# Moving the last stores of a DMA-bound attention backward pass onto chosen DMA engines

## The chip, the cores and the metric

The kernel runs on one core of a Trainium2 chip. The metric is the device time of one execution in microseconds (us); lower is better. Executions of the kernel before on one chip lie within 0.2%. Times in a trace count from the start of the span; the span is about 1.8 us shorter than the time (400.8 against 402.56 us for the profiled run of the kernel before).

## The reference, cut to what matters

The program is the forward and backward pass of one decode step: 32 heads attend over a cache of 4096 keys and values of width 128, beside a small gated MLP. Its outputs include the gradients of both caches, which are as large as the caches.

```python
def _A_ref(x, k_cache, v_cache, wq, wo):          # B, Sq = 1, 1; D = 640
    q = (x @ wq).reshape(B, Sq, H, Dh).transpose(0, 2, 1, 3)
    scores = jnp.einsum("bhqd,bhkd->bhqk", q, k_cache) * (Dh ** -0.5)
    o = jnp.einsum("bhqk,bhkd->bhqd", softmax(scores), v_cache)
    return o.transpose(0, 2, 1, 3).reshape(B, Sq, H * Dh) @ wo
# ... g * A + (1 - g) * B, with B an MLP
# outputs: the result, and d/d(x, k_cache, v_cache, wq, wo, w1, b1, w2, gate_w)
```

K and V are read (32 MB each), dK and dV are written (32 MB each), and the weights and their gradients make up the rest of 165 MB.

## The kernel before

Per head, K and V (1 MB each) are loaded by SyncE, and dK and dV (1 MB each) are stored by GpSimd; the last stores go through SyncE. A DMA "engine" below is one of the core's 16; the traces don't name them. The parts that the change touches:

```python
def ring(h):
    return nc.sync if h >= H - 2 else nc.gpsimd
...
        def dwo():                                   # one of 8 tiles of d(wo), 128 x 5120 B
            for i in range(G):
                nc.vector.tensor_scalar(wos[g][:, i, :], da_bc[:], fs["o4"][:, i:i + 1], None, ALU.mult)
            (nc.sync if g == NG - 1 else nc.gpsimd).dma_start(dwo_v[g], wos[g][:])
...
        if h == H - 1:                               # dK of the last head, in two halves
            a, b = half * (J // 2), (half + 1) * (J // 2)
            ring(h).dma_start(dKv[h][:, a:b, :], st["dK"][:, a:b, :])
...
        if half == 1:
            if h % 7 == 5 and h < H - 3:             # heads 5, 12, 19, 26
                spread(h // 7, dVv[h], st["dV"])
            else:
                ring(h).dma_start(dVv[h], st["dV"][:])

    def spread(i, dst, t):                           # a dV store meant to nearly skip one engine
        ...
        if i % 3 == 0:
            nc.gpsimd.inc_swdge_sem([], [], mode="reset_dge_cursor")
        for a, b in (((120, 125), (0, 120), (125, 128)), ((0, 14), (14, 119), (119, 128)), ((0, 8), (8, 128)))[i % 3]:
            nc.gpsimd.dma_start(out[a:b, :], src[a:b, :], max_dma_last_dim=J * Dh)
...
    nc.sync.dma_start(dwq_v[:, :, CL:], dwq_l[:])    # the last columns of d(wq)
...
    for i, dst in enumerate((out0_rows, out1_rows, out9_rows)):
        nc.scalar.dma_start(dst, fin_rows[i * RC:(i + 1) * RC, :])    # small results, last of all
```

Of the kernel before, what the change touches and what calls it, by code (L numbers as in the profile page):

```python
# [16 lines left out]
def kernel(  # L17
# [24 lines left out]
    nc = tc.nc  # L42
    P = 128
    _, H, Sk, Dh = A_k_cache.shape
# [6 lines left out]
    NG = H // G  # L51
# [15 lines left out]
    dKv = out_2.rearrange("b h (p j) d -> (b h) p j d", p=P)  # L67
    dVv = out_3.rearrange("b h (p j) d -> (b h) p j d", p=P)
    wq_v = A_wq.rearrange("(rc r) c -> r rc c", r=P)
    dwq_v = out_4.rearrange("(rc r) c -> r rc c", r=P)  # L70
    wo_v = A_wo.rearrange("(g p i) n -> g p i n", p=P, i=G)
    dwo_v = out_5.rearrange("(g p i) n -> g p i n", p=P, i=G)
# [26 lines left out]
    def f32v(ap):  # L99
        return ap.bitcast(F32)  # L100

    def bcast_rows(out, cols, n, parts=P):
        for i in range(n):
            nc.tensor.transpose(out[:, i, :], cols[:, i:i + 1].to_broadcast([parts, P]),
                                ident_bf[0:parts, 0:parts])
# [7 lines left out]
    kts, vts, wqs, wos = {}, {}, {}, {}  # L113

    def ring(h):
        return nc.sync if h >= H - 2 else nc.gpsimd
# [132 lines left out]
    def add(name, kind, fn, deps=(), head=0):  # L249
        steps.append((name, kind, fn, tuple(deps), head))  # L250
# [83 lines left out]
    def finish_steps(g):  # L334
        fs = {}

        def om():
            fs["om"] = small.tile([P, G, G], BF16, name="om", tag="om")
            nc.vector.tensor_tensor(fs["om"][:], o_all[:, g * G:(g + 1) * G].unsqueeze(2).to_broadcast([P, G, G]),
                                    mask4[:].to_broadcast([P, G, G]), ALU.mult)  # L340

        def o4():
            fs["ps"] = gr_ps.tile([P, G], F32, name="o4_ps", tag="gr")
            R = P // G
            for hh in range(G):
                nc.tensor.matmul(fs["ps"][hh * R:(hh + 1) * R, :], lhsT=red4[:], rhs=fs["om"][:, hh, :],
                                 start=True, stop=True)

        def o4c():
            fs["o4"] = small.tile([P, G], F32, name="o4", tag="o4")  # L350
            nc.vector.tensor_copy(fs["o4"][:], fs["ps"][:])
            fs["o4b"] = small.tile([P, G], BF16, name="o4b", tag="o4b")
            nc.vector.tensor_copy(fs["o4b"][:], fs["o4"][:])

        def amm():
            fs["ap"] = gr_ps.tile([P, RC], F32, name="ap_ps", tag="gr")
            for c in range(RC):
                for i in range(G):
                    nc.tensor.matmul(fs["ap"][:, c:c + 1], lhsT=wos[g][:, i, c * P:(c + 1) * P],
                                     rhs=fs["o4b"][:, i:i + 1], start=(i == 0), stop=(i == G - 1))  # L360

        def aadd():
            nc.vector.tensor_tensor(a_acc[:], a_acc[:], fs["ap"][:], ALU.add)

        def dwo():
            for i in range(G):
                nc.vector.tensor_scalar(wos[g][:, i, :], da_bc[:], fs["o4"][:, i:i + 1], None, ALU.mult)  # L367
            (nc.sync if g == NG - 1 else nc.gpsimd).dma_start(dwo_v[g], wos[g][:])

        def dqb():  # L370
            b_ps = gr_ps.tile([P, G, P], BF16, name="b_ps", tag="gr")
            bcast_rows(b_ps, dq_all[:, g * G:(g + 1) * G], G)
            nc.scalar.copy(f32v(dq_bc[:, g * GD:(g + 1) * GD]), f32v(b_ps[:].rearrange("p a b -> p (a b)")))

        def dx(rc, c0, c1, slot_i):
            def f():
                w = g // 2
                nc.vector.scalar_tensor_tensor(junk[:, c0:c1], in0=wqs[w][:, rc, c0:c1], scalar=1.0,  # L378
                                               in1=dq_bc[:, w * WG * Dh + c0:w * WG * Dh + c1],
                                               op0=ALU.mult, op1=ALU.mult, accum_out=dxp[:, rc, slot_i:slot_i + 1])  # L380
            return f

        n = lambda x: f"{x}{g}"
        add(n("om"), "T", om)
        add(n("dqb"), "P", dqb)
        add(n("o4"), "P", o4, (n("om"),))
        add(n("o4c"), "T", o4c, (n("o4"),))
        add(n("amm"), "P", amm, (n("o4c"),))
        add(n("aadd"), "T", aadd, (n("amm"),))
        add(n("dwo"), "D", dwo, (n("aadd"),))  # L390
        for rc in range(RC):
            if g >= NG - 2:
                add(n(f"dx{rc}_"), "D", dx(rc, (g % 2) * GD, (g % 2 + 1) * GD, g - NG + 2 + NW - 1), (n("dqb"),))
            elif g % 2 == 1:
                add(n(f"dx{rc}_"), "D", dx(rc, 0, WG * Dh, g // 2), (n("dqb"),))
# [206 lines left out]
    def outer(dst, col, row, half):  # L602
        n = J // 2
        a, b = half * n, (half + 1) * n
        nc.vector.tensor_tensor(  # L605
            dst[:, a:b, :].rearrange("p j (a b) -> p j a b", b=2),
            col[:, a:b, :].unsqueeze(2).to_broadcast([P, n, Dh // 2, 2]),
            row.rearrange("p (a b) -> p a b", b=2).unsqueeze(1).to_broadcast([P, n, Dh // 2, 2]),
            ALU.mult)

    def dk_half(h, half):
        if h < 0:
            return
        st = sts[h]
        if half == 0:
            st["dK"] = outs.tile([P, J, Dh], BF16, name="dK_sb", tag="dVK")
        outer(st["dK"], st["ds"], gps[h // G]["qd"][:, 0, (h % G) * Dh:(h % G + 1) * Dh], half)
        if h == H - 1:
            a, b = half * (J // 2), (half + 1) * (J // 2)
            ring(h).dma_start(dKv[h][:, a:b, :], st["dK"][:, a:b, :])  # L620
        elif half == 1:
            ring(h).dma_start(dKv[h], st["dK"][:])  # L622
        if half == 1:
            sts.pop(h)

    def dv_half(h, half):
        st = sts[h]
        if half == 0:
            st["dV"] = outs.tile([P, J, Dh], BF16, name="dV_sb", tag="dVK")
        outer(st["dV"], st["p"], gps[h // G]["qd"][:, 1, (h % G) * Dh:(h % G + 1) * Dh], half)  # L630
        if half == 1:
            if h % 7 == 5 and h < H - 3:
                spread(h // 7, dVv[h], st["dV"])
            else:
                ring(h).dma_start(dVv[h], st["dV"][:])  # L635

    def spread(i, dst, t):
        src = t[:].rearrange("p j d -> p (j d)")
        out = dst.rearrange("p j d -> p (j d)")
# [5 lines that stand above are left out]
    def period(h):  # L645
# [12 lines left out]
        def o_part(a, b):  # L658
            for j in range(a, b):
# [4 lines left out]
        nc.vector.reduce_max(m32[:], S, axis=AX.X)  # L664
        V(0)
        dk_half(h - 1, 0)
        V(1)
        nc.tensor.transpose(MM, m32[:].to_broadcast([P, P]), ident_f[:])
        negM = small.tile([P, 1], F32, name="negM", tag="negM")
        nc.vector.tensor_reduce(negM[:], MM, axis=AX.X, op=ALU.max, negate=True)  # L670
        dk_half(h - 1, 1)
        e = st["e"] = small.tile([P, J], BF16, name="e_bf", tag="e_bf")
        V(2)
# [17 lines left out]
        nc.vector.scalar_tensor_tensor(pj[:], in0=DP[:, 0:J], scalar=1.0, in1=e[:], op0=ALU.mult, op1=ALU.mult,  # L691
                                       accum_out=part[:])
        dv_half(h, 0)
        nc.tensor.transpose(PT, part[:].to_broadcast([P, P]), ident_f[:])  # L694
        if nxt:
# [6 lines left out]
        nc.vector.scalar_tensor_tensor(ds[:], in0=DP[:, 0:J].unsqueeze(2).to_broadcast([P, J, 2]), scalar=dd[:], in1=p_bf[:],  # L702
                                       op0=ALU.subtract, op1=ALU.mult)
        dv_half(h, 1)
        nc.vector.tensor_scalar(o_all[:, h:h + 1], O[:, 0:1], rz[:], None, ALU.mult)  # L705
        if nxt:
# [20 lines left out]
    CL = (NG - 1) * GD  # L727
# [21 lines left out]
    for h in range(H):  # L749
        hh, g = h % G, h // G  # L750
# [21 lines left out]
        if hh == G - 1:  # L772
            mlp_left = steps[:]
            steps.clear()
            finish_steps(g)
            steps.extend(mlp_left)
    dk_half(H - 1, 0)
    dk_half(H - 1, 1)
    last = [st for st in steps if st[0].startswith("dx")]
# [3 lines left out]
    dwq_l = wts.tile([P, RC, GD], BF16, name="dwq_l", tag="wo_g", bufs=3)  # L783
    for rc in range(RC):
        nc.vector.tensor_scalar(dwq_l[:, rc, :], dq_bc[:, CL:], x_f[:, rc:rc + 1], None, ALU.mult)
    nc.sync.dma_start(dwq_v[:, :, CL:], dwq_l[:])
    assert len(dwqt) == RC and stored

# [65 lines left out]
```

## Time and profile before

The time is 402.4 us (402.1 to 402.5).

| | before |
|---|---|
| bytes moved | 164.92 MB |
| mean rate over the span | 412 GB/s |
| busiest compute engine (DVE) | 76% |
| rate from 380 to 385 us | 426 GB/s |
| rate from 395 us to the end | 121 GB/s |

The head of the profile page of the kernel before shows the busy time of each engine, and below it the span in 40 equal slices: the busy share of the DMA engines in tenths, and the rate.

```profile
span 400.8 us, 13361 instructions
PE 301.0 (75%) x5752; PEld 266.0 (66%) x5752; DVE 303.1 (76%) x783; ACT 178.2 (44%) x403; POOL 47.0 (12%) x94
DMA  8999999999999999999999999999999999999995
GB/s 292 417 407 405 418 426 421 407 423 421 424 421 424 422 422 416 422 424 424 419 424 426 422 422 417 417 425 424 421 421 424 424 423 418 425 420 418 424 383 229
```

No compute engine is full, and the DMA engines are busy from the second slice to the last but one: the kernel is bound by DMA, and only the tail has room. The windows view of the tail gives, per stretch of time, the busy time and instruction count of PE, PEld, DVE, ACT and POOL, then the clock granted to PE, the share of busy DMA engines, and GB/s.

```profile
380.00:385.00 5.00, 0.45 (x1) 0.18 (x1) 4.82 (x22) 0.00 (x0) 0.00 (x0) 0.50 1.02 426
385.00:390.00 5.00, 0.28 (x1) 0.09 (x1) 2.38 (x9) 0.25 (x1) 0.00 (x0) 0.50 0.86 358
390.00:395.00 5.00, 0.00 (x0) 0.00 (x0) 0.00 (x0) 0.00 (x0) 0.00 (x0) 0.50 0.91 360
395.00:401.00 6.00, 0.00 (x0) 0.00 (x0) 0.00 (x0) 0.00 (x0) 0.00 (x0) 0.50 0.32 121
```

Up to 385 us all engines work; then some run dry. The timeline of the same stretch (start, length, issuing queue, line, transfer, count) and the waits of SyncE (who waited for what: total us, times, longest) show the last stores being issued.

```profile
374.79 2.55 SPq L736 DMA_DIRECT2D out_dram<-dwq_t  x2
377.43 2.48 SPq L620 DMA_DIRECT2D out_dram<-dK_sb  x2
388.20 1.43 ACTq L824 DMA_DIRECT2D out_dram<-fin_rows  x3
389.73 0.33 SPq L368 DMA_DIRECT2D out_dram<-wo_g  x1
391.90 0.38 SPq L786 DMA_DIRECT2D out_dram<-dwq_l  x1
```

```profile
SPq L368 <- DMA out_dram<-dV_sb: 9.8, 1, 9.8
SPq L786 <- DMA out_dram<-dwq_t: 1.8, 1, 1.8
```

The last dwo tile (wo_g, line 368) waits 9.8 us for a dV store that has nothing to do with its data. The transfers of the two hardware rings (SyncE's and ACT's) take turns on eight completion semaphores in the trace (100, 102 to 106, 109 and 110, 12 or 13 transfers on each). In this program a store is issued only when the transfer that last used its semaphore has landed: the last update of that dV store is at 389.66 us, and dwo is issued at 389.73; dwq_l is issued at 391.90, after the dwq_t store on its semaphore has landed at 391.83.

How uneven the 16 DMA engines are can be read from the semaphore updates in the trace: 16 for each of these stores, taken here as one per engine. They don't name the engine, but sorted they give this, in us, for the last stores of the kernel before (worked out from the trace; "early" are the six engines ahead, "late" the ten behind):

```
second half of dK   early 387.96 388.06 388.08 388.11 388.19 390.16   late 393.30 ... 396.53
dwo                 early 392.49 ... 392.68                          late 394.85 ... 398.07
dwq_l               early 395.06 ... 395.21                          late 396.52 ... 399.67
```

### The profile page before, as it was taken

How to read it: one execution, taken by the hardware profiler on the slowest of the kernel's cores; microseconds unless marked ns; L12 is line 12 of the kernel's file. 1: busy time of each engine (PE TensorE's matmuls, PEld its weight loads, DVE VectorE, ACT ScalarE, POOL GpSimd, SP SyncE). 2: the span in 40 equal slices, each digit the busy share in tenths (PEclk: the TensorE clock that was granted, in tenths of full speed). 3: DMA queues.
4: the chain of work that ended last, by engine and by line, in shares of the span. 5: the costliest groups of instructions: out<-in, count | busy, mean ns of one | idle time of the engine just before them, and what ended most of it. 6: DMA issues, size and time to landing. Idle time of an engine off the chain costs nothing.

```text
span 400.8 us, 13361 instructions
## 1 busy us (share of the span) xinstructions
PE 301.0 (75%) x5752; PEld 266.0 (66%) x5752; DVE 303.1 (76%) x783; ACT 178.2 (44%) x403; POOL 47.0 (12%) x94
## 2 busy tenths in 40 slices
PE   0788888678888788768879788838888888888300
PEld 0577888567777677658868778718777678877200
DVE  3339666556799999767658999836999997898860
ACT  1455454325545555326533555604545545555000
POOL 0001111021110111211110112101111121111000
PEclk9899999959999999969977999967999999999755
DMA  8999999999999999999999999999999999999995
GB/s 292 417 407 405 418 426 421 407 423 421 424 421 424 422 422 416 422 424 424 419 424 426 422 422 417 417 425 424 421 421 424 424 423 418 425 420 418 424 383 229
DMA packets 28359, 164.92 MB, mean 412 GB/s; under 512 B 3260, under 2 KB 3964, under 8 KB 12556
## 3 DMA queue, kind: packets, MB, share of 16 engines
q1 hardware_dynamic: 17136, 93.41, 56.5%
q0 software_dynamic: 11104, 70.64, 42.3%
q8 instruction: 45, 0.74, 0.7%
q14 instruction: 14, 0.11, 0.1%
q10 hardware_dynamic: 60, 0.01, 0.0%
HBM read 82.03 MB, written 82.03 MB: 409 GB/s over the span
## 4 chain that ended last, share of the span: by engine, by line
DVE 38%; DMA 32%; PE 20%; ACT 5%; issue 3%; ACTq 0%; SPq 0%
DMA Kn<-in_A_k_cache_dram 30%; DVE dK_sb L605 9%; DVE dV_sb L605 9%; PE tr L580 8%; DVE junk L378 5%; ACT tT L582 4%; DVE junk L278 3%; PE sA L660 3%; PE sA L589 3%; PE sB L713 3%; DVE junk L530 2%; DVE wo_g L367 1%; DMA vec_rows<-in_gate_w_dram 1%; DVE dj L700 1%; DVE dwq_t L732 1%
## 5 line engine op out<-in xcount | busy, mean ns | idle before, releaser
L582 ACT COPY tT<-tr 128x512 f32<-128x512 f32 x256 | 142.4, 587 | 127.8 <-PE tr L580 126.0
L589 PEld LDWEIGHTS <-tT 128*128 128x128 bf16 x2048 | 79.8, 98 | 40.3 <-ACT tT L582 34.6
L580 PE MATMUL tr<-ident_f,Kn 128*128 128x128 f32 x512 | 81.6, 297 | 9.2 <-DMA Kn<-in_A_k_cache_dram 9.2
L605 DVE TENSOR_TENSOR dV_sb<-p_bf,qd 128x2048 bf16<-128x2048 bf16 x64 | 78.0, 1218 | 0.2 <-issue 0.2
L605 DVE TENSOR_TENSOR dK_sb<-ds_bf,qd 128x2048 bf16<-128x2048 bf16 x64 | 77.7, 1216 | 0.0
L580 PE MATMUL tr<-ident_f,Vn 128*128 128x128 f32 x512 | 72.9, 278 | 0.0
L580 PEld LDWEIGHTS tr<-ident_f,Kn 128*128 128x128 f32 x512 | 61.0, 152 | 10.4 <-issue 10.4
L589 PE MATMUL sA<-qd,tT 128*128 128x48 bf16 x1024 | 48.7, 187 | 23.8 <-ACT dq_all L718 12.7
L580 PEld LDWEIGHTS tr<-ident_f,Vn 128*128 128x128 f32 x512 | 56.3, 142 | 0.0
L589 PE MATMUL sB<-qd,tT 128*128 128x48 bf16 x1024 | 46.0, 183 | 0.0
L660 PEld LDWEIGHTS <-Vn 128*128 128x128 bf16 x1024 | 30.2, 95 | 10.9 <-issue 10.9
L660 PE MATMUL sA<-e_bf,Vn 128*128 128x48 bf16 x1024 | 30.7, 183 | 8.1 <-DVE zs L680 6.5
L622 POOL DMA_DIRECT2D out_dram<-dK_sb x30 | 17.2, 574 | 138.9 <-DVE rz L682 86.5
L713 PE MATMUL sB<-ds_bf,Kn 128*128 128x48 bf16 x1024 | 32.2, 186 | 1.4 <-DVE ds_bf L702 1.4
L664 DVE TENSOR_REDUCE m<-sA 128x1 f32<-128x32 f32 x32 | 6.1, 189 | 32.9 <-PE sA L589 26.4
L713 PEld LDWEIGHTS <-Kn 128*128 128x128 bf16 x1024 | 29.5, 98 | 1.6 <-issue 1.6
L635 POOL DMA_DIRECT2D out_dram<-dV_sb x26 | 14.1, 542 | 135.8 <-DVE o_all L705 53.4
L278 DVE SCALAR_TENSOR_TENSOR junk<-wo_g,da_bc 128x640 bf16<-128x640 bf16 x32 | 26.2, 820 | 1.7 <-ACT da_bc L229 1.1
L378 DVE SCALAR_TENSOR_TENSOR junk<-wq_g,dq_bc 128x1024 bf16<-128x1024 bf16 (+1 forms) x25 | 25.1, 1005 | 0.2
L700 DVE TENSOR_SCALAR_CACHE_REDUCE dj<-sB,rz 128x128 f32<-128x128 f32 x32 | 11.1, 346 | 13.2 <-PE sB L694 13.2
L289 PE MATMUL q_ps<-wq_g,cols_bf 128*128 128x512 bf16 x40 | 13.1, 469 | 10.5 <-DMA wq_g<-in_A_wq_dram 10.5
L684 ACT ACTIVATE p_bf<-e_bf,rz 128x64 bf16<-128x64 bf16 x32 | 11.1, 348 | 13.9 <-DVE rz L682 11.1
(148 smaller groups left out, 268.8 us busy)
## 6 DMA issues: line engine op xcount, KB each, us to landing
Kn<-in_A_k_cache_dram SPq DMA_DIRECT2D x32, 1024.0 KB, 24.0
Vn<-in_A_v_cache_dram SPq DMA_DIRECT2D x32, 1024.0 KB, 28.0
out_dram<-dK_sb POOLq DMA_DIRECT2D x30, 1024.0 KB, 11.8
out_dram<-dV_sb POOLq DMA_DIRECT2D x26, 1024.0 KB, 11.8
wq_g<-in_A_wq_dram SPq DMA_DIRECT2D x4, 1280.0 KB, 23.2
wo_g<-in_A_wo_dram SPq DMA_DIRECT2D x8, 640.0 KB, 17.6
out_dram<-wo_g POOLq DMA_DIRECT2D x7, 640.0 KB, 11.8
out_dram<-dwq_t SPq DMA_DIRECT2D x4, 896.0 KB, 17.5
```

Source lines behind the costliest of these rows:

```text
L278: nc.vector.scalar_tensor_tensor(junk[:, 0:D], in0=wos[g][:, i, :], scalar=1.0, in1=da_bc[:], op0=ALU.mult, op1=ALU.mult, accum_out=gp["do ...
L289: nc.tensor.matmul(q_ps[:], lhsT=x_bf[:, rc:rc + 1].to_broadcast([P, P]), rhs=wq[:, rc, off:off + GD], start=(rc == 0), stop=(rc == RC - 1))
L378: nc.vector.scalar_tensor_tensor(junk[:, c0:c1], in0=wqs[w][:, rc, c0:c1], scalar=1.0, in1=dq_bc[:, w * WG * Dh + c0:w * WG * Dh + c1], op ...
L580: nc.tensor.transpose(tp[:, t, :], flat[:, k * P:(k + 1) * P], ident_f[:])
L582: nc.scalar.copy(sb[:].rearrange("p a b -> p (a b)"), tp[:].rearrange("p a b -> p (a b)"))
L589: nc.tensor.matmul(out[:, 2 * k:2 * k + W], lhsT=tb[:, t, par, :], rhs=vec[:, par, :].unsqueeze(1).to_broadcast([P, W // 2, 2]), start=(pa ...
L605: nc.vector.tensor_tensor(dst[:, a:b, :].rearrange("p j (a b) -> p j a b", b=2), col[:, a:b, :].unsqueeze(2).to_broadcast([P, n, Dh // 2, 2]),
L622: ring(h).dma_start(dKv[h], st["dK"][:])
L635: ring(h).dma_start(dVv[h], st["dV"][:])
L660: nc.tensor.matmul(O, lhsT=vts[h][:, j, :], rhs=st["e"][:, j:j + 1].to_broadcast([P, W]), start=(j == 0), stop=(j == J - 1))
L700: nc.vector.tensor_scalar(dj[:], PT, rz[:], None, ALU.mult, ALU.add, accum_out=dd[:])
L713: nc.tensor.matmul(DQ, lhsT=kts[h][:, j, :], rhs=ds[:, j, 0:1].to_broadcast([P, W]), start=(j == 0), stop=(j == J - 1))
```

## The change

The intent is to give the engines that run dry early more of the last bytes and the late ones fewer, to relieve one late engine by two more dV stores that are meant to nearly skip it, and to keep dwo and dwq_l out of SyncE's waits by using ACT's ring.

```diff
-            (nc.sync if g == NG - 1 else nc.gpsimd).dma_start(dwo_v[g], wos[g][:])
+            if g == NG - 1:
+                for a, b in ((0, 124), (124, P)):
+                    nc.scalar.dma_start(dwo_v[g][a:b], wos[g][a:b])
+            else:
+                nc.gpsimd.dma_start(dwo_v[g], wos[g][:])
@@ dK of the last head
-            ring(h).dma_start(dKv[h][:, a:b, :], st["dK"][:, a:b, :])
+            for rows in ([slice(c, 108, 4) for c in range(4)] + [slice(108, P)] if half else [slice(0, P)]):
+                nc.sync.dma_start(dKv[h][rows, a:b, :], st["dK"][rows, a:b, :])
@@ dV
-            if h % 7 == 5 and h < H - 3:
-                spread(h // 7, dVv[h], st["dV"])
+            if h % 4 == 0 and 0 < h < H - 7:
+                spread(h // 4 - 1, dVv[h], st["dV"])
@@ the last columns of d(wq)
-    nc.sync.dma_start(dwq_v[:, :, CL:], dwq_l[:])
+    nc.scalar.dma_start(dwq_v[:, :, CL:], dwq_l[:])
```

The traces show how many engines a store lands on. On the two rings a store of 128 rows shows 16 semaphore updates. In the changed kernel the stores of 124 and of 4 rows show four updates, those of 27 rows nine, that of 20 rows ten and those of 5 rows (fin_rows) five, each beside one more that comes 0.16 to 0.42 us after the end of the issue and is taken here for the issuing queue's own. Which engines these are isn't shown. This text calls the groups the four (dwo), the five (fin_rows), the nine and the ten (small dK stores). The recorded texts call them engines 0 to 3, 0 to 4, 0 to 8 and 0 to 9; these numbers are names only, and that each group contains the smaller ones is assumption.

## The prediction

> **What bounds the kernel now.** The DMA engines. The profile page gives 164.92 MB at a mean 412 GB/s, and a DMA share of nine tenths or more in nearly every slice; the windows view gives a share of 1.00 to 1.02 and 417 to 426 GB/s up to 385 us. DVE (76%), PE (75%) and ACT (44%) have slack. Only the tail leaves the DMA engines idle: 358 and 360 GB/s in 385 to 395 us and 121 GB/s in 395 to 401 us, against about 424.
>
> The semaphore updates in the trace (one per engine) show why. The second half of the last dK lands at 388.0 us on five engines, 390.2 on a sixth and 393.3 to 396.5 on ten. The last dwo, computed by 380.7 us (timeline), is issued only at 389.7, because SyncE waits 9.8 us for an earlier dV store (waits view, SyncE): it reuses that store's semaphore. dwq_l follows at 391.9 and lands at 395.1 on the six and 396.5 to 399.7 on the ten. Averaging the ends that the engines would have without that idle time gives 395.8 (an estimate), so perfect balance is worth at most about 3.9 us: 1%.
>
> **What the change does.** No byte is added. [...] At 26.3 GB/s an engine (32 KB in 1.25 us):
> - dwo: engines 0 to 3 +4.7 us each, the others -1.56 us.
> - Half of dK: 0 to 8 +0.94 us, 9 -0.94, 10 to 15 -1.25.
> - Two more dV stores that nearly skip one engine [...]: -4.0 us there, +0.3 us elsewhere. Their 4,096 B packets take 159 ns against 309 per 8,192 B: 0.1 us.
> - dwo and dwq_l on ACT's ring start near 381 and 382.6 us and interleave with SyncE's: the idle time at 388 to 391 us goes.
>
> The late engines among 10 to 15 thus end 2.8 us earlier.
>
> **What takes part of it back.** fin_rows goes to engines 0 to 4 and lands at once on only three, late on two: so one of engines 0 to 3 may be a late one and get 5.9 us more. And the five small dK stores reuse semaphores: in the built program they wait for the last dK store but one, the small dwo store, the last big dwq store, dwq_l and the first half of dK. The last of them should start only at 396 to 398 us and land 1 to 2 us later. The third fin_rows store waits for dwo.
>
> **Prediction.** All of it lies on the tail, which is the critical path; expected gain 1.9 us of the 3.9. Time 400.5 us, range 398.3 to 402.8. Faster by over 2%: 0.01; within 2%: 0.98; slower by over 2%: 0.01.
>
> **What would show it.** Right: until 380 us unchanged rates and busy times; no wait of SyncE before dwo; dwo issued by ACT near 381 us; 385 to 390 us at 400 GB/s or more; in the waits view SyncE waiting for dwo, dwq_t or dwq_l before the small dK stores, some microseconds in total; these last dK pieces or fin_rows the last to land. Wrong: the dK stores issued without waits, the last landing being dwo.
>
> **What would make it wrong.** Engines 0 to 3 all early and short waits: 398 us. A late engine among them, or the dK pieces serialised behind dwq_l: 402 us or more. The waits of POOL for its three-part stores holding dV buffers longer.

No term of its sum is cut: it came to a gain of 1.9 us of the 3.9, so to 400.5 us. The shifts per engine are estimates from bytes at 26.3 GB/s, which is a 16th of the 421 GB/s that the page shows in many slices. The packet times are medians of the trace of the kernel before (159 and 309 ns). That the two dV stores nearly skip one engine was assumption. Which engines are among "10 to 15", and that the late ones are there, wasn't shown.

## The result, and the profile after

The time went up to 407.6 us (406.4 to 407.8). The ratio to the kernel before is 1.0125, with a 95% interval from 1.0110 to 1.0141. Ratios here are the mean time of one kernel's fast runs over that of the other's of the same rounds, so not quite the ratio of the medians that are quoted. Outputs are correct.

The same parts of the page of the changed kernel:

```profile
span 406.0 us, 13363 instructions
PE 299.2 (74%) x5745; PEld 265.2 (65%) x5752; DVE 302.5 (75%) x783; ACT 178.2 (44%) x403; POOL 49.5 (12%) x97
DMA  8999999999999999999999999999999999999982
GB/s 289 419 408 399 421 425 417 420 424 424 419 422 422 423 423 416 416 429 423 421 424 419 425 421 419 414 427 422 422 424 420 427 420 424 421 420 419 417 325 80
```

Bytes are the same and the engines' busy times nearly so; the loss is in the last two slices. The windows of the tail (same columns as before):

```profile
380.00:385.00 5.00, 0.45 (x1) 0.18 (x1) 4.75 (x21) 0.00 (x0) 0.00 (x0) 0.50 1.00 412
385.00:390.00 5.00, 0.28 (x1) 0.09 (x1) 1.05 (x5) 0.26 (x1) 0.00 (x0) 0.50 0.97 390
390.00:395.00 5.00, 0.00 (x0) 0.00 (x0) 0.00 (x0) 0.00 (x0) 0.00 (x0) 0.50 0.82 283
395.00:400.00 5.00, 0.00 (x0) 0.00 (x0) 0.00 (x0) 0.00 (x0) 0.00 (x0) 0.50 0.37 130
400.00:406.00 6.00, 0.00 (x0) 0.00 (x0) 0.00 (x0) 0.00 (x0) 0.00 (x0) 0.50 0.20 62
```

From 385 to 390 us more is moved than before (390 against 358 GB/s), as wanted. After 395 us the DMA engines are busy for 0.37 and then 0.20 of the time, and for 11 us instead of 6. The timeline of the issues and SyncE's waits:

```profile
379.36 1.51 ACTq L370 DMA_DIRECT2D out_dram<-wo_g  x2
381.81 0.33 SPq L741 DMA_DIRECT2D out_dram<-dwq_t  x1
383.96 0.41 ACTq L791 DMA_DIRECT2D out_dram<-dwq_l  x1
386.06 17.02 SPq L625 DMA_DIRECT2D out_dram<-dK_sb  x6
391.45 6.16 ACTq L829 DMA_DIRECT2D out_dram<-fin_rows  x3
```

```profile
SPq L625 <- DMA out_dram<-wo_g: 8.5, 1, 8.5
SPq L741 <- DMA out_dram<-dV_sb: 7.3, 1, 7.3
SPq L625 <- DMA out_dram<-dwq_t: 3.9, 1, 3.9
SPq L625 <- DMA out_dram<-dwq_l: 2.5, 1, 2.5
SPq L625 <- DMA out_dram<-dK_sb: 2.0, 1, 2.0
```

dwo leaves at 379.4 us instead of 389.7. But dK, whose two last stores left within 2.5 us before, now goes as six stores that leave over 17 us: the third waits 8.5 us for the small dwo store, the fifth 2.5 us for dwq_l. The landing times say why those waits last so long (from the semaphore updates, us):

```
dwo (4 engines)              392.08  394.84  395.52  397.32
dwq_l (16 engines), last 6   397.09  397.35  397.72  397.76  400.62  401.83
fourth small dK store        404.11 ... 404.39   (issued after dwq_l had landed)
fifth small dK store         404.50 ... 404.71   (the last landing of all; before: 399.67)
```

Two engines are 3 and 4 us behind the 14 others with dwq_l, and the last dK stores wait for them. Which two can be told in part. fin_rows runs on five engines and follows dwq_l on ACT's ring; four of the first store's five updates come 0.17 or 0.18 us after one of dwq_l's, taken here for the same engine's (395.40 after 395.22, 397.52 after 397.35, 397.89 after 397.72, 400.80 after 400.62; also 402.26 after 402.08 in the run with dK whole below). None follows that of 401.83: all three fin_rows stores had landed by 401.19. So the engine of 400.62 is one of the five, and the last one, at 401.83, is not.

### The profile page after: what moved, and what is told of

Same layout as the page of the kernel before. It is cut to its first block, busy times and chain, and to the rows that moved or that the text cites. A ratio compares the mean times of both kernels' runs of the same rounds, so it can differ in the third digit from the quotient of the medians.

```text
span 406.0 us, 13363 instructions
## 1 busy us (share of the span) xinstructions
PE 299.2 (74%) x5745; PEld 265.2 (65%) x5752; DVE 302.5 (75%) x783; ACT 178.2 (44%) x403; POOL 49.5 (12%) x97
## 4 chain that ended last, share of the span: by engine, by line
DVE 36%; DMA 29%; PE 20%; ACT 6%; issue 3%; ACTq 0%
DMA Kn<-in_A_k_cache_dram 28%; DVE dK_sb L609 9%; DVE dV_sb L609 8%; PE tr L584 8%; ACT tT L586 5%; DVE junk L382 5%; PE sA L665 4%; PE sA L593 3%; PE sB L718 2%; DVE junk L278 2%; DVE junk L534 1%; DMA vec_rows<-in_gate_w_dram 1%; DVE wo_g L367 1%; DVE dj L705 1%; DVE junk L491 1%
## 5 line engine op out<-in xcount | busy, mean ns | idle before, releaser
L640 POOL DMA_DIRECT2D out_dram<-dV_sb x24 | 13.1, 546 | 139.1 <-DVE dV_sb L609 58.6
L289 PE MATMUL q_ps<-wq_g,cols_bf 128*128 128x512 bf16 x33 | 11.7, 474 | 15.6 <-DMA wq_g<-in_A_wq_dram 14.9
L292 ACT CAST qd<-q_ps 128x512 bf16<-128x512 f32 x8 | 4.7, 586 | 31.1 <-PE q_ps L289 31.1
```

The source lines that it names most:

```text
L289: nc.tensor.matmul(q_ps[:], lhsT=x_bf[:, rc:rc + 1].to_broadcast([P, P]), rhs=wq[:, rc, off:off + GD], start=(rc == 0), stop=(rc == RC - 1))
```

## The experiments

Theory A: the small dK stores wait for unrelated stores, because they reuse their semaphores. Theory B: one of the four engines of dwo was a late one, and four-engine dwo overloads it. Rival C: the six three-part dV stores cost time of their own. Rival D: ACT's ring disturbs the tail. Each run is compared with the kernel before on the same chip: the first four shared a chip, as did the next four (four-engine dwo alone to no waits with dwo on 16) and the next three (the probe, half the dose, nine engines); the last had its own. The changed kernel was not run again beside them, so comparisons with it, and between groups, go through the ratios.

### The six dV stores alone

Kernel before, with this edit only:

```diff
-            if h % 7 == 5 and h < H - 3:
-                spread(h // 7, dVv[h], st["dV"])
+            if h % 4 == 0 and 0 < h < H - 7:
+                spread(h // 4 - 1, dVv[h], st["dV"])
```

> [...] Theory A (the small dK stores wait for other stores because they reuse their semaphores) and theory B (dwo on four engines overloads a late one of them) both say that this part is harmless: 401.0 to 403.0 us, SyncE's wait before dwo stays near 10 us. Rival C (the three-part dV stores cost time of their own): 404 us or more, with DMA rates under 415 GB/s before 380 us.

Measured: 402.36 us (ratio 1.0007, 0.9983 to 1.0030). C falls. The relief does reach an engine. The fin_rows stores run on five engines. Following the packets backward from each engine's last one (a packet starts where the one before on its engine ends; a reconstruction of mine from the packet records) puts the last packet of the latest of these five at 399.31 us before and at 396.29 us here. It bought nothing, because five other engines still ended at 398.5 to 399.1 us.

### dwo and dwq_l from ACT's ring alone

```diff
-            (nc.sync if g == NG - 1 else nc.gpsimd).dma_start(dwo_v[g], wos[g][:])
+            (nc.scalar if g == NG - 1 else nc.gpsimd).dma_start(dwo_v[g], wos[g][:])
-    nc.sync.dma_start(dwq_v[:, :, CL:], dwq_l[:])
+    nc.scalar.dma_start(dwq_v[:, :, CL:], dwq_l[:])
```

> The kernel before with the last dwo (whole, on 16 engines) and the last dwq columns issued by ACT, nothing else: no four-engine store, no small dK stores. A and B: 398.0 to 400.5 us, since the idle time of the six early engines at 388 to 391 us goes and nothing is added. Under a rival D (ACT's ring itself disturbs the tail by interleaving) 403 us or more.

Measured: 402.48 us (ratio 1.0000, 0.9983 to 1.0017). This is a miss, and the most instructive one. D falls, but so does the gain. The windows of this run:

```profile
385.00:390.00 5.00, 0.28 (x1) 0.09 (x1) 0.93 (x5) 0.26 (x1) 0.00 (x0) 0.50 1.02 414
390.00:395.00 5.00, 0.00 (x0) 0.00 (x0) 0.00 (x0) 0.00 (x0) 0.00 (x0) 0.50 0.72 293
395.00:401.00 6.00, 0.00 (x0) 0.00 (x0) 0.00 (x0) 0.00 (x0) 0.00 (x0) 0.50 0.31 124
```

The early engines no longer run dry at 388 us: 414 GB/s instead of 358. They only do the same work earlier and run dry at the end instead (293 instead of 360). The ten late engines had work queued all that time in the kernel before (they landed dK at 393.3 to 396.5 us, after dwo was issued at 389.7), have the same bytes here and end at the same time: the last landing is at 399.38 us (399.67 before).

### dK whole again, dwo still on four engines

The changed kernel, with this edit:

```diff
-            for rows in ([slice(c, 108, 4) for c in range(4)] + [slice(108, P)] if half else [slice(0, P)]):
-                nc.sync.dma_start(dKv[h][rows, a:b, :], st["dK"][rows, a:b, :])
+            ring(h).dma_start(dKv[h][:, a:b, :], st["dK"][:, a:b, :])
```

> The changed kernel with the last half of dK stored whole again (dwo still on four engines). If A is the whole loss: 399 to 401 us. If B is a part of it as well: 402.5 to 405 us, dwq_l landing last at about 401 us after the start on one of the four engines. If C: above 406 us.

Measured: 405.42 us (ratio 1.0065, 1.0050 to 1.0080). A is not the whole loss: without the small dK stores 0.65% of 1.25% is left. The 16 landings of dwq_l end with 398.18, 398.63, 399.36 and 402.08 us: one engine alone is 2.7 us behind the next, and it is one of the five, since a fin_rows update follows it at 402.26.

### dwo on 16 engines, the five dK stores kept

```diff
-                for a, b in ((0, 124), (124, P)):
-                    nc.scalar.dma_start(dwo_v[g][a:b], wos[g][a:b])
+                nc.scalar.dma_start(dwo_v[g], wos[g][:])
```

> The changed kernel with dwo stored whole by ACT on 16 engines (the five dK stores stay, and still wait for dwo, dwq_l, a dwq store and the first half of dK). If A is the whole loss: still 406 us or more. If B is a part: 401 to 404 us, because dwo and dwq_l land some 3 to 5 us earlier, and the waits of SyncE before the dK stores shrink from 17 us to about 12, but do not vanish.

Measured: 404.24 us (ratio 1.0045, 1.0026 to 1.0064), slightly above the range of 401 to 404 us that was expected if B is a part, but well under 406. With four engines taken away, 0.8% goes (1.0125 to 1.0045); what stays is the waiting of the small stores, the third of which left at 396.72 us, when dwq_l had landed at 396.70:

```profile
SPq L737 <- DMA out_dram<-dV_sb: 8.4, 1, 8.4
SPq L621 <- DMA out_dram<-dwq_l: 8.0, 1, 8.0
SPq L621 <- DMA out_dram<-dwq_t: 5.2, 2, 2.8
```

### Four-engine dwo alone

The edit of dwo in the change, alone, on the kernel before.

> The kernel before with the last dwo stored by engines 0 to 3 from ACT's ring, and nothing else. Theory B (one of these four is a late engine; its tail ended at 396.2 us before and gets 4.7 us more): about 401 us for the last landing, 403.5 to 405 us in all. Theory A (only the semaphore waits before the small dK stores matter): as before, 401.5 to 403 us.

Measured: 404.68 us (ratio 1.0061, 1.0030 to 1.0092), as B said. But it is not B pure. Here dwq_l is still SyncE's, and it reused the semaphore of dwo; the waits of SyncE show it:

```profile
SPq L790 <- DMA out_dram<-wo_g: 13.5, 1, 13.5
```

dwq_l left at 399.2 us, after dwo had landed on its last engine. So A's mechanism plays a part even here, through another store. The profiled run had a granted clock of 0.728 against 0.92 in the others, and dwo was issued at 383.36 us, not 379.4, so the wait in this trace may not be that of the other three runs.

### Five dK stores alone

The edit of dK in the change, alone, on the kernel before.

> The kernel before with the last half of dK in five stores, and nothing else. dwo and dwq_l are still SyncE's and queue behind the five, whose last waits for the first half of dK to land on its slowest engine (395.3 us). Theory A: dwo and dwq_l start only after 395.5 us and need 3.1 us on every engine and 1 us to land, so 404 to 407 us, with over 18 us of waits on SyncE in the tail. If only B matters: 401.5 to 403 us.

The 3.1 us are an estimate: twice 40 KB an engine at 26.3 GB/s. The 1 us is about what fin_rows took from its first issue (388.20 us) to its first landing (389.33) in the kernel before.

Measured: 403.83 us (ratio 1.0033, 1.0017 to 1.0050): a real loss, a little under the range that A gave. dwo left at 395.84 us and dwq_l at 396.31, and then all 16 engines worked on them together and landed within 0.3 us of each other (400.62 to 400.84). So waiting also had the effect of lining the engines up; the last landing is 1.2 us later than before.

This trace also shows how many of the engines that got more of dK were late. The first small store runs on nine engines and landed on five of them at 387.00 to 389.37 us, on the other four at 392.33, 393.17, 394.48 and 395.77. The last is 0.46 us after the latest of the 16 landings of the half of dK before it (395.31). So four of the nine were late, and the latest engine of all was among them.

### The changed kernel without the waits

The five dK stores are issued by GpSimd, which has eight semaphores of its own (111 to 118 in the trace of the changed kernel). The edit was meant to keep the bytes on the same engines; that isn't shown.

```diff
-            for rows in ([slice(c, 108, 4) for c in range(4)] + [slice(108, P)] if half else [slice(0, P)]):
-                nc.sync.dma_start(dKv[h][rows, a:b, :], st["dK"][rows, a:b, :])
+            if half == 0:
+                nc.sync.dma_start(dKv[h][:, a:b, :], st["dK"][:, a:b, :])
+            else:
+                for rows in [slice(c, 108, 4) for c in range(4)] + [slice(108, P)]:
+                    nc.gpsimd.inc_swdge_sem([], [], mode="reset_dge_cursor")
+                    nc.gpsimd.dma_start(dKv[h][rows, a:b, :].rearrange("p j d -> p (j d)"),
+                                        st["dK"][rows, a:b, :].rearrange("p j d -> p (j d)"),
+                                        max_dma_last_dim=J // 2 * Dh)
```

> The changed kernel with the five dK stores issued by GpSimd[...]; its semaphores have long been free, so they don't wait. [...] A: the last 3 us go, and what is left is B alone: the late engine of the four ends near 402 us, total 404.5 to 406 us. If A were the whole loss: 399 to 401 us. If the waits did not matter: 407 us or more.

Measured: 406.31 us (ratio 1.0096, 1.0081 to 1.0111). The timeline shows that the stores left without waiting:

```profile
375.60 3.18 POOL L629 DMA_DIRECT2D out_dram<-dK_sb  x5 [15.29 <-DVE om L339]
378.36 1.42 ACTq L370 DMA_DIRECT2D out_dram<-wo_g  x2
383.15 0.41 ACTq L797 DMA_DIRECT2D out_dram<-dwq_l  x1
```

So taking the waits away gave back 0.3% (1.0125 to 1.0096, about 1.2 us; the two intervals just touch), less than half of the 3 us expected. This is no clean measure of the waits, since the stores also moved to another queue and to an earlier time. A large part of the rest stays with the four: dwo landed on them at 396.9, 397.6, 398.9 and 399.9 us, and dwq_l landed last at 402.81. The fin_rows stores, which queue behind dwo and dwq_l on ACT's ring, landed at 395.57 on one of the five and at 399.04 to 402.99 on the four others. The one at 395.57 landed before dwo had landed anywhere, which fits an engine on which dwo has no bytes; the latest engine is then one of the four.

### No waits, and dwo on 16 engines

> As the run without waits, and dwo on 16 engines: neither A nor B is left[...]. A and B together explain the whole loss if this is at 400.5 to 402.5 us, under the kernel before or level with it; above 403 us something else is at work.

The edits are those of the two runs "without the waits" and "dwo on 16 engines" together. Measured: 403.69 us (402.80 to 404.67; ratio 1.0032, 1.0011 to 1.0052): a miss. With both causes gone, 0.9 of the 1.25% is gone, but the kernel isn't level with the one before. In its trace, the fastest of its four runs, the last landing is at 399.50 us; fin_rows had landed on its five engines by 397.80, so the last engine was none of these. The kernel that would tell what the five dK stores cost here, the same with dK whole, was not run.

### Which engine is late

The kernel before, with the small result rows stored in other groups. A store on few engines is used to tell by its landing times how many of them are free.

```diff
-    for i, dst in enumerate((out0_rows, out1_rows, out9_rows)):
-        nc.scalar.dma_start(dst, fin_rows[i * RC:(i + 1) * RC, :])
+    for i, dst, cuts in ((0, out0_rows, (0, 2, 5)), (1, out1_rows, (0, 1, 5)), (2, out9_rows, (0, 5))):
+        for a, b in zip(cuts, cuts[1:]):
+            nc.scalar.dma_start(dst[a:b], fin_rows[i * RC + a:i * RC + b, :])
```

> The kernel before with its small result rows stored in groups of 2, 3, 1, 4 and 5 rows[...]. On an early engine such a store lands within 1 us, on a late one 2 to 4 us later. Theory B expects exactly one late engine among 0 to 3 and engine 4 late too; the rival (all four early, engine 4 and another late) none among the stores of 2, 3 and 4 rows.

One look, 402.87 us. The semaphore updates of the five stores (us; each store shows one update more than it has rows, and the first, 0.43 us after the issue, is taken here for the issuing queue's own):

```
2 rows                    387.54 | 388.21  390.12
3 rows                    387.85 | 388.52  388.55  390.30
1 row                     388.15 | 388.82
4 rows                    390.56 | 391.23  391.25  391.26  393.22
5 rows                    394.87 | 395.53  395.54  395.55  395.60  398.46
```

Beside that one, each store shows as many updates as it has rows. Read by the number of rows, the engine of the one-row store answers 0.67 us after the queue's own update, so it is free. Of the two engines of the two-row store the other answers at 390.1, when the sixth of the early engines has ended the dK store (389.94 us in this trace). Of three engines two are free at once. Of four, three are free, and one answers 2.7 us after the queue's own update. Of five, four are free by then, and one answers 3.6 us after it. If each store runs on the engines of the smaller ones and one more, which fits but isn't shown, then the fourth row adds a late engine ("engine 3"), and the fifth row another ("engine 4"). So one of the four was late, and dwo in the change gave it the same 123 KB more as the three others.

### Half the dose on the four engines

The changed kernel with dK whole and this edit: 68 rows of dwo in one store, meant for the four engines, and 60 in another, meant for 15.

```diff
-                for a, b in ((0, 124), (124, P)):
+                for a, b in ((0, 68), (68, P)):
```

> The changed kernel with dK whole and of dwo only 68 rows on engines 0 to 3 [...]: 2.6 us more on each of the four instead of 4.7. B (dose on one late engine): the last landing 2.1 us or more before that of the whole-dK run with all of dwo on four engines (402.6 us in its trace), so near 400 us, total 402.3 to 403.5 us. If the four-engine form as such costs: 404.5 us or more.

The 2.6 and 4.7 us are estimates from bytes at 26.3 GB/s, and 2.6 assumes those numbers of engines.

Measured: 403.12 us (ratio 1.0007, 0.9988 to 1.0026). The loss falls with the dose: 1.0065 with all of dwo on four engines, 1.0007, no loss clear of noise, with about half of it. The last landing moves from 402.64 to 400.72 us.

### dwo on nine engines

The changed kernel with dK whole and dwo in stores of 63, 63 and 2 rows, the larger two meant for nine engines.

> The changed kernel with dK whole and dwo on engines 0 to 8 (two stores of 63 rows, one of 2): 1.2 us more on each of the nine[...]. If balance alone decides: 400.5 to 402 us. If stores on fewer engines than 16 slow packets as much as they save: 402.5 to 404 us.

Measured: 403.88 us, but the four runs are 402.01, 402.99, 406.00 and 404.77, and the ratio 1.0037 has the interval 0.9995 to 1.0078. This is inconclusive; the profiled run, the fastest, ended its last landing at 398.99 us.

### dwo meant for the three engines that are free

The changed kernel with dK whole, and dwo in stores of 69 rows (meant for the three engines that the probe showed free; that it ran on these isn't shown), 48 (for all) and 11 (for 11).

```diff
-                for a, b in ((0, 124), (124, P)):
+                for a, b in ((0, 69), (69, 117), (117, P)):
```

> The changed kernel with dK whole and dwo put on engines that the probe showed not to be late: [...] Theory B (only the late engine 3 made the four-engine store costly): the loss of 3 us of the whole-dK run is gone, 401.0 to 402.4 us. If a store on few engines costs by its form (packets slowed on every engine): 403.5 us or more.

Measured: 401.76 us (401.50 to 402.09), ratio 0.9982 (0.9968 to 0.9995). It differs from the whole-dK run only in how dwo is cut, and so in which engines were meant to carry it, and 3.7 us of difference in the medians lie between them (0.83% by the ratios, since the chips differ). It is the one version here that beats both kernels, by 0.2%: clear of noise, if small. Its last landing is at 398.49 us. The tail of its windows:

```profile
385.00:390.00 5.00, 0.10 (x1) 0.00 (x0) 0.00 (x0) 0.26 (x1) 0.00 (x0) 0.50 0.96 385
390.00:395.00 5.00, 0.00 (x0) 0.00 (x0) 0.00 (x0) 0.00 (x0) 0.00 (x0) 0.50 0.90 356
395.00:400.00 5.00, 0.00 (x0) 0.00 (x0) 0.00 (x0) 0.00 (x0) 0.00 (x0) 0.50 0.27 104
```

From 390 to 395 us it keeps 0.90 of the DMA engines busy, where the changed kernel had 0.82, and after that less is left.

### All runs together

| run | engines of dwo | last half of dK | ratio to before |
|---|---|---|---|
| six dV stores alone | 16, SyncE | whole | 1.0007 |
| ACT's ring alone | 16, ACT | whole | 1.0000 |
| the change | four | five, with waits | 1.0125 |
| no waits | four | five, GpSimd | 1.0096 |
| dK whole | four | whole | 1.0065 |
| dwo on 16 | 16 | five, with waits | 1.0045 |
| no waits, dwo on 16 | 16 | five, GpSimd | 1.0032 |
| half dose | 68 rows for four | whole | 1.0007 |
| three free engines | 69 rows for three | whole | 0.9982 |
| dwo on nine | for nine | whole | 1.0037, unclear |
| four-engine dwo alone | four, dwq_l by SyncE | whole | 1.0061 |
| five dK stores alone | 16, SyncE | five, with waits | 1.0033 |
| the probe | 16, SyncE | whole | one look, 402.87 us |

## Why the prediction was wrong

The prediction said 400.5 us, with a range up to 402.8; the time was 407.6. Point by point:

- **"What bounds the kernel now" was right.** The rates before 380 us and the busy times hardly changed (from 385 to 390 us it reached 390 GB/s, not the 400 forecast); all of the loss is in the tail: at 390 us 2.44 MB was left to move, against 2.53 MB before (worked out from the windows), and the deficit comes after that.
- **The step that failed is the sum: "All of it lies on the tail, which is the critical path; expected gain 1.9 us of the 3.9".** The 3.9 us came from averaging the ends of 16 engines, but the tail ends with its latest engine. "the idle time at 388 to 391 us goes" was true and worth nothing: in the run of ACT's ring alone that idle time went and the time stayed (ratio 1.0000), because it was idle time of engines that were not last.
- **"-4.0 us there" was also worth nothing by itself** (1.0007): the latest of five engines ended 3.0 us earlier in the reconstruction, but five others did not.
- **"one of engines 0 to 3 may be a late one and get 5.9 us more" named the main cause and left it out of the sum, as a "may".** The probe shows one late engine among four. Four-engine dwo against dwo on 16 engines is 0.80% with the waits (1.0125 against 1.0045) and 0.64% without (1.0096 against 1.0032): 2.6 to 3.2 us. With dK whole, the loss is gone with the store cut to half the dose (1.0007) or to 69 rows meant for the three free engines (0.9982). The hint had been in the trace of the kernel before: fin_rows had landed late on two of its five engines (392.37 and 392.53 us, the others by 390.33).
- **"the five small dK stores reuse semaphores" was right in mechanism and wrong in size.** The stores named in the prediction are the ones in the waits view. But the last of them was said to start "at 396 to 398 us" and left at 402.6, because it stands behind the one that waits for dwq_l, and dwq_l landed last at 401.83. In this trace that was not on the late one of the four: the latest of the five landed it at 400.62, and the last engine is none of them. The first small dK store, which runs on nine engines, also landed last at 401.63, so it may be one of the nine, but that isn't shown. Issuing the five stores without waits gave back 0.3%, dropping them 0.60% (1.0125 to 1.0065).
- **"The late engines among 10 to 15 thus end 2.8 us earlier" left out those elsewhere.** The dK part of the change moved bytes to nine engines, and in the run of five dK stores alone four of these nine were late (392.33 to 395.77 us), among them the latest of all.
- **"At 26.3 GB/s an engine" did not hold for the stores on few engines.** The packets of dwo (5,120 B) took 196 ns each, nearly without exception, when ACT's ring stored it on 16 engines in the run of that ring alone; the mean was 199 ns in the kernel before and 208 ns with the five dK stores alone. On four engines the median was still 196 ns, but some took 400 or more, and the mean was 212 ns in the changed kernel, 245 ns in the run without waits and 254 ns in the run of four-engine dwo alone; packets of other stores grew as well (7,168 B on SyncE's ring: 272 to 291 ns in the run without waits). All packets of the span together took 399.1 us an engine before, 399.3 with dK whole, 399.0 with three free engines, 400.7 in the change and 400.9 without waits: some 1.6 to 1.8 us more for the same bytes where four-engine dwo meets the five dK stores. That may hide part of what the waits cost. These figures are worked out from the packet records. The prediction had no term for it.

What stays open: why packets slow in these runs, and whether the few engines are the cause. Also open is why the run without either cause is at 1.0032 rather than level with the kernel before; the late engines among the nine, which were meant to get more of dK there too, are a suspicion that no run tests. The run of three free engines has the six dV stores, ACT's ring and the new dwo at once; how its 0.2% divides among them was not tried.

## What to carry to other kernels

When a queue-bound kernel ends raggedly, find out which engine ends last before moving bytes: taking away idle time from engines that are not last was worth nothing here (ratio 1.0000), and one late engine in the group that gets more can turn the gain into a loss (2.6 to 3.2 us for four-engine dwo). Very small stores, of one to five rows, told here in one look how many of their engines were free (0.67 us after the queue's own update, against 2.7 us). Before a store is split into pieces, see which semaphore each piece takes and which store held it before: in this kernel the pieces waited up to 8.5 us for stores that had nothing to do with them, and the last piece stood behind one that waited for dwq_l on its latest engine (401.83 us).
